# Row-tiled memory products of a query pair: tiles of 64 by 64 in place of 64 by 128

## The chip, the cores and the metric

The kernel runs on one core of one Trainium2 chip. The metric is the device time of one execution in microseconds (us). Before the change three runs took 629.06 us in the median (628.87 to 629.29).

## What is computed

Attention with a compressive memory feeds a gated feed-forward layer. There are 4 batches of 8 heads with 576 positions of 64 elements; the feed-forward layer has 2304 rows of 512, 1536 hidden units, and all weights arrive as 64-bit floats.

```python
scores = scale * np.matmul(q, k.transpose(0, 1, 3, 2))          # causal
a = softmax(scores)
local = np.matmul(a, v)
q_p = phi(q)                                                    # elu(q) + 1
mem_ret = np.einsum('bhsd,bhde->bhse', q_p, M_prev)
mem_norm = np.einsum('bhsd,bhd->bhs', q_p, z_prev)[..., None] + 1e-06
attn = g * mem_ret / mem_norm + (1 - g) * local
gate = 1.0 / (1.0 + np.exp(-(x @ w_gate)))
out = (gate * (x @ w_val)) @ w_out
```

`mem_ret` and `mem_norm` together are the memory products: 64 rows of features against 65 columns (64 of `M_prev` and one of `z_prev`) for each head.

## The kernel before

The 2304 rows go in 6 groups of 384. Four groups are the first 384 positions of one batch each; two groups (the first and the last that are worked on) are the "tails", the last 192 positions of two batches together. Each group has 4 pairs of heads, so there are 16 plain pairs and 8 tail pairs. A pair's two heads lie in SBUF partitions 0 to 63 and 64 to 127, and a product over 64 elements of one head uses only half the rows of the TensorE array. Such products run row-tiled: head 0 in the upper half of the array and head 1 in the lower half, each into its own PSUM bank. Between them the array works untiled on the products of the feed-forward layer (`matmul`, recorded on L313), on transposes (L320) and on the products with the values (`product`, L317, tiles of 128 by 64).

A row-tiled visit is one block: `scores` writes it with `pg.block()`, and all its instructions stand together in TensorE's queue. `heads` (L561) issues the score products of the visit. For one visit of each pair `more` is true; then `terms` (L518) adds the pair's memory products behind the scores, into the free columns of the same two banks. For a plain pair this is the visit `x == 0`, with one block of 128 queries against 256 keys, and memory products for three blocks of 128 queries. A tail pair's visit with `more` has two cells of 64 queries, one of each batch, each into its own half of the PSUM partitions, and its memory products are in cells of 64 queries too.

Each float32 matmul of the program stands as two matmul records with two weight loads in the trace (two passes).

After a visit DVE reads the scores of each bank with its mask and takes the row extremum (L623), ACT makes the exponentials (L635), and `recall` (L500, L504, L336 `xm`) divides the memory products by their norms. While the first plain group is in work, each hidden block's weights are turned from 64-bit floats into pairs of float32 values: `convert` loads a piece, ACT scales it (L805), DVE shifts and merges it (L807, L809, L812), ACT rounds it (L326) and DVE takes the rest (L336). There are three pieces for each of the 12 hidden blocks. Later groups load the converted weights back.

The order of all instructions comes from a planner (`Program.issue`). Each operation has an engine, an estimated cost in us and dependencies; the planner simulates the queues with these costs, and in 800 rounds of a seeded random search it moves operations that let TensorE wait in its model earlier, and keeps an order whose modelled end isn't later. The cost that a visit is given there is

```python
pe(4 * at / 2385.0 + (0.63 if more else 0.3), together, ...)
```

where `at` is the number of score columns. It costs nothing on the chip by itself; it is one input of the order.

Of the kernel before, what the change touches and what calls it, by code (L numbers as in the profile page):

```python
# [238 lines left out]
def tile_attention_memory_moe(  # L239
# [62 lines left out]
    def bank(kind):  # L302
        ids = {"att": att_banks, "gv": [3, 4], "second": [0, 1]}[kind]
        turns[kind] += 1
        t, k = banks[ids[(turns[kind] - 1) % len(ids)]]
        return t, pg.renew(k)

    def pe(cost, emit, r, w):
        pg.add("pe", cost, emit, r, w)

    def matmul(out, lhsT, rhs, n, r, w, start, stop):
        pe(0.004 + max(n, 128) / 2250.0,
           lambda: nc.tensor.matmul(out=out, lhsT=lhsT, rhs=rhs, start=start, stop=stop), r, w)  # L313
# [8 lines left out]
    def act(n, emit, r, w):  # L322
        pg.add("act", 0.09 + n / 1200.0, emit, r, w)
# [4 lines left out]
    def dve(n, emit, r, w, fast=False):  # L328
        pg.add("dve", 0.065 + n / (1920.0 if fast else 960.0), emit, r, w)
# [179 lines left out]
    def terms(u, sp, js, at):  # L509

        for c in range(3):
            cells = [(0, 128 * c, 0, 128)]
            if u.tail:
                es = (0, 1) if c == 2 else (c, c)
                cells = [(e, e * TL + (128 if c == 2 else m0), m0, m0 + 64) for e, m0 in zip(es, (0, 64))]
            for e, q, m0, m1 in cells:
                for j, r in enumerate(js):
                    nc.tensor.matmul(  # L518
                        out=sp[j][0][m0:m1, at + MC * c:at + MC * c + MC], lhsT=u.ph[r, q:q + m1 - m0],
                        rhs=mem[u.g][e][0][r, u.p, MC * j:MC * j + MC], start=True, stop=True)  # L520

    def recall(n, parts):

        u = pairs[n]
        xm, xk = xm_r.take()
        scaled(xm, [xk], parts, rn_r, 1e-6, gs[:, 2 * u.p:2 * u.p + 2], "gs")
        u.xm, u.xm_k = xm, [xk]

    def divided(u):

        return u.tail and u.n >= HP
# [24 lines left out]
    def heads(u, es, sp, js, k0, k1, at):  # L556

        for e, q, m0, m1 in es:
            kp, _ = u.kp[e]
            for j, r in enumerate(js):  # L560
                nc.tensor.matmul(  # L561
                    out=sp[j][0][m0:m1, at:at + k1 - k0], lhsT=kp[r, u.qa + q:u.qa + q + m1 - m0],
                    rhs=kp[r, u.ka + k0:u.ka + k1], start=True, stop=True)

    def scores(n, x):

        u = pairs[n]
        pair = u.tail and x == 2
        js = [slice(64 * j, 64 * j + 64) for j in range(2)]
        a = [a_r.take() for _ in js]  # L570
        if pair:
            _, q0, W = u.items[x][0]
            parts = [[(0, 0, 320)], [(0, 320, W)]]
        else:
            parts = [[(i, 0, W) for i, (_, _, W) in enumerate(u.items[x])]]
        st = [[st_r.take() for _ in js] for _ in u.items[x]]

        def part(i, cells):
            sp = [bank("att") for _ in js]
            more = pair and i == 1 or not u.tail and x == 0  # L580
            work, at = [], 0
            for y, k0, k1 in cells:
                c, q0, W = u.items[x][y]
                if pair:
                    es = [(0, 128, 0, 64), (1, 128, 64, 128)]
                    mk, mk_k = (mask2[:, :k1 - k0], "mask2") if i else (mask[:, :k1 - k0], "mask")
                else:
                    es = [(c if u.tail else 0, q0, 0, 128)]
                    mk, mk_k = mask[:, 512 - W:], "mask"
                work.append((y, es, k0, k1, at, mk, mk_k))  # L590
                at += k1 - k0
            if more:
                u.told = [(sp[j][0][:, at:at + 3 * MC].rearrange("p (c j x) -> p c j x", c=3, j=1),
                           sp[j][1], j, j + 1) for j in range(2)]

            def together():
                for _, es, k0, k1, o, _, _ in work:
                    heads(u, es, sp, js, k0, k1, o)
                if more:
                    terms(u, sp, js, at)  # L600

            with pg.block():
                if not divided(u) or pair:
                    e_ = {e for _, es, *_ in work for e, *_ in es}
                    pe(4 * at / 2385.0 + (0.63 if more else 0.3), together,
                       [u.kp[e][1] for e in e_] + (u.ph_k + [k for _, mk in mem[u.g] for k in mk] if more else []),
                       [sp[j][1] for j in range(2)])
                else:
                    (_, es, k0, k1, _, _, _), = work
                    m = k1 - k0  # L610
                    for j in range(2):
                        kq, kk, ql, kx = u.kq[j][es[0][0]]
                        keys = kq[:, u.ka + k0:u.ka + k1]
                        out, out_k = sp[j][0][:, :m], sp[j][1]
                        q = es[0][1]
                        matmul(out, kq[:, u.qa + q:u.qa + q + 128], keys, m, kk, [out_k], True, False)
                        matmul(out, ql[:, q:q + 128], keys, m, kk + kx, [out_k], False, True)
            for y, es, k0, k1, o, mk, mk_k in work:
                m = k1 - k0
                b0 = 0 if pair else sum(W for _, _, W in u.items[x][:y])  # L620
                for j in range(2):
                    (aj, ak), (sj, sk), (pj, pk) = a[j], st[y][j], sp[j]
                    dve(m + 60, lambda aj=aj, sj=sj, pj=pj, o=o, m=m, mk=mk, b=b0 + k0: nc.vector.tensor_tensor_reduce(  # L623
                        out=aj[:, b:b + m], in0=pj[:, o:o + m], in1=mk, scale=-0.125,
                        scalar=3.0e38 if i == 0 else sj[:, i - 1:i],
                        op0=ALU.add, op1=ALU.min, accum_out=sj[:, i:i + 1],
                    ), [pk, mk_k] + [sk] * (i > 0), [ak + (y,), sk])

        for i, cells in enumerate(parts):
            part(i, cells)  # L630
        u.a[x] = []
        b0 = 0
        for y, (_, _, W) in enumerate(u.items[x]):
            for (aj, ak), (sj, sk) in zip(a, st[y]):
                act(W + 120, lambda aj=aj, sj=sj, b=b0, W=W: nc.scalar.activation(  # L635
                    out=aj[:, b:b + W], in_=aj[:, b:b + W], func=AF.Exp, scale=-1.0,
                    bias=sj[:, len(parts) - 1:len(parts)],
                ), [ak + (y,), sk], [ak + (y,)])
            b0 += W
        u.a[x] = [(aj, [ak + (y,) for y in range(len(u.items[x]))], ak) for aj, ak in a]  # L640
        if u.told:
            recall(n, u.told)
            u.told = None
# [382 lines left out]
```

## Time and profile before

| | us |
|---|---|
| median of 3 runs | 629.06 |
| the profiled execution | 629.38 |
| its span | 627.5 |
| TensorE matmuls busy (PE) | 610.7 (97%) |
| weight loads busy (PEld) | 535.5 (85%) |
| VectorE (DVE) | 409.8 (65%) |
| ScalarE (ACT) | 267.5 (43%) |

The profile shows one execution. PE and PEld are TensorE's matmuls and its weight loads, which overlap. The ends of matmul records are modelled and records overlap, so what an instruction costs is read from the distance between starts. In the timeline, equal instructions that follow each other are merged into one row with their count.

### The profile page before, as it was taken

To read this page: it belongs to the slowest core of one execution; us is meant where nothing else is said; L and a number is where in the kernel's file an instruction comes from. 1 tells how busy PE (TensorE), PEld (TensorE's weight loads), DVE (VectorE), ACT (ScalarE), POOL (GpSimd) and SP (SyncE) were. 2 spreads that over 40 slices of the span, in tenths; PEclk is the share of its full clock that TensorE was granted. 3 is DMA by queue.
4 is the path that set the end of the run, shared out by engine and by line. 5 is a ranking of instruction groups with operands and counts; after the bars stand their busy time and mean duration, and the time that the engine had idled before them with its cause. 6 is when DMAs were issued, how large, how long until landed. Compare 5 with 4: busy or idle time off the path is not lost.

```text
span 627.5 us, 12396 instructions
## 1 busy us (share of the span) xinstructions
PE 610.7 (97%) x4928; PEld 535.5 (85%) x4928; DVE 409.8 (65%) x1091; ACT 267.5 (43%) x536; POOL 9.5 (2%) x51
## 2 busy tenths in 40 slices
PE   6889999998999999999999999999999999999996
PEld 3559888986898988898988898988898989999995
DVE  4999999998865568756566756678697573121211
ACT  6997667756533324333242434246363221211111
POOL 2000000000000000000000000000000000000000
PEclk9999999999999999999999999999999999999999
DMA  8667878796499699668786467978668994225351
GB/s 303 231 229 240 270 283 276 249 311 225 93 281 297 210 217 254 116 174 216 187 219 209 107 173 211 223 203 229 139 147 219 181 218 146 100 84 191 146 194 57
DMA packets 103130, 126.42 MB, mean 201 GB/s; under 512 B 79648, under 2 KB 81696, under 8 KB 95776
## 3 DMA queue, kind: packets, MB, share of 16 engines
q1 hardware_dynamic: 102928, 125.36, 69.7%
q8 instruction: 39, 0.64, 0.4%
q10 hardware_dynamic: 144, 0.26, 0.1%
q14 instruction: 19, 0.16, 0.1%
HBM read 89.43 MB, written 17.30 MB: 170 GB/s over the span
## 4 chain that ended last, share of the span: by engine, by line
PE 90%; DVE 6%; DMA 1%; ACT 1%; issue 1%; DVEq 0%; ACTq 0%
PE bank L313 72%; PE bank L317 7%; PE bank L561 6%; PE bank L320 2%; PE bank L518 2%; DVE a L623 1%; DMA wr<-in_w_dram 1%; DVE wt L809 1%; DVE wt L812 1%; ACT a L635 1%; DVE sv L336 1%; DMA kp<-in_qk_dram 1%; DVE wt L807 0%; DVE ph L492 0%; ACT wt L805 0%
## 5 line engine op out<-in xcount | busy, mean ns | idle before, releaser
L313 PE MATMUL bank<-xh,wg 128*128 128x384 f32 x576 | 163.4, 341 | 2.2 <-ACT wg L326 2.0
L313 PE MATMUL bank<-xh,sv 128*128 128x384 f32 x576 | 164.1, 341 | 0.3 <-DVE th L897 0.2
L313 PE MATMUL bank<-sv,gh 128*128 128x512 f32 x432 | 136.2, 396 | 0.3 <-ACT gh L326 0.3
L313 PEld LDWEIGHTS bank<-xh,wg 128*128 128x128 f32 x576 | 104.8, 188 | 8.8 <-ACT wg L326 2.8
L313 PEld LDWEIGHTS bank<-xh,sv 128*128 128x128 f32 x576 | 104.8, 188 | 2.8 <-DVE sv L336 0.7
L897 DVE SCALAR_TENSOR_TENSOR th<-th,bank 128x384 f32<-128x384 f32 x72 | 39.7, 551 | 98.0 <-PE bank L313 96.9
L313 PE MATMUL bank<-xl,wg 128*128 128x384 f32 x288 | 97.8, 340 | 0.0
L313 PE MATMUL bank<-xl,sv 128*128 128x384 f32 x288 | 97.6, 339 | 0.0
L313 PEld LDWEIGHTS bank<-sv,gh 128*128 128x128 f32 x432 | 79.5, 188 | 14.2 <-ACT gh L326 0.7
L895 ACT ACTIVATE th<-bank 128x384 f32<-128x384 f32 x72 | 35.3, 490 | 131.0 <-PE bank L313 130.8
L635 ACT ACTIVATE a<-a,st 128x256 f32<-128x256 f32 (+4 forms) x144 | 77.3, 581 | 26.9 <-DVE st L623 26.3
L623 DVE CUSTOM_DVE_ANT_0 a<-bank,mask 128x256 f32<-128x256 f32 (+3 forms) x144 | 64.9, 485 | 36.3 <-PE bank L561 18.3
L313 PE MATMUL bank<-sv,gl 128*128 128x512 f32 x216 | 84.8, 396 | 0.0
L326 ACT CAST gh<-th 128x384 fp32r<-128x384 f32 x72 | 36.9, 513 | 104.7 <-DVE th L897 104.5
L313 PEld LDWEIGHTS bank<-xl,wg 128*128 128x128 f32 x288 | 54.1, 188 | 4.1 <-issue 1.0
L561 PE MATMUL bank<-kp 64*128 64x256 f32 (+4 forms) x352 | 52.5, 452 | 4.0 <-DMA kp<-in_qk_dram 4.0
L653 DVE COPY at<-tl_wr 128x1024 uint16<-128x1024 uint16 (+1 forms) x72 | 46.8, 654 | 12.7 <-DMA tl_wr<-pl_wr 12.5
L313 PEld LDWEIGHTS bank<-xl,sv 128*128 128x128 f32 x288 | 54.1, 188 | 0.5
L336 DVE TENSOR_TENSOR gl<-th,gh 128x384 fp32r<-128x384 f32 x72 | 39.8, 554 | 15.5 <-ACT gh L326 15.2
L313 PEld LDWEIGHTS bank<-sv,gl 128*128 128x128 f32 x216 | 40.5, 188 | 9.4 <-DVE gl L336 0.4
L649 DVE COPY pl_wr<-a 128x1024 uint16<-128x1024 uint16 (+1 forms) x72 | 41.8, 593 | 3.8 <-ACT a L635 3.8
L561 PEld LDWEIGHTS bank<-kp 64*128 64x128 f32 (+1 forms) x352 | 23.1, 169 | 23.8 <-issue 10.5
(66 smaller groups left out, 588.0 us busy)
## 6 DMA issues: line engine op xcount, KB each, us to landing
sv<-w SPq DMA_DIRECT2D x45, 1024.0 KB, 5.4
wr<-in_w_dram SPq DMA_DIRECT2D x36, 512.0 KB, 4.6
kp<-in_qk_dram SPq DMA_DIRECT2D x32, 384.0 KB, 4.1
w<-sv SPq DMA_DIRECT2D x12, 1024.0 KB, 6.6
out_dram<-ob SPq DMA_DIRECT2D x14, 256.0 KB, 2.2
vt<-in_vp_dram SPq DMA_DIRECT2D x8, 330.0 KB, 4.8
vr<-in_vp_dram SPq DMA_DIRECT2D x8, 330.0 KB, 4.1
mb<-in_mz_dram SPq DMA_DIRECT2D x8, 260.0 KB, 3.5
```

What stands on the lines that cost most here:

```text
L313: lambda: nc.tensor.matmul(out=out, lhsT=lhsT, rhs=rhs, start=start, stop=stop), r, w)
L317: lambda: nc.tensor.matmul(out=out, lhsT=lhsT, rhs=rhs, start=start, stop=stop), r, w)
L320: pe(0.110, lambda: nc.tensor.transpose(out=out, in_=in_, identity=identity), r, w)
L326: act(n, lambda: nc.scalar.copy(out=out, in_=in_), r, w)
L336: dve(n, lambda: nc.vector.tensor_tensor(out=out, in0=in0, in1=in1, op=op), r, w)
L561: nc.tensor.matmul(out=sp[j][0][m0:m1, at:at + k1 - k0], lhsT=kp[r, u.qa + q:u.qa + q + m1 - m0], rhs=kp[r, u.ka + k0:u.ka + k1], start=Tr ...
L623: dve(m + 60, lambda aj=aj, sj=sj, pj=pj, o=o, m=m, mk=mk, b=b0 + k0: nc.vector.tensor_tensor_reduce(out=aj[:, b:b + m], in0=pj[:, o:o + m ...
L635: act(W + 120, lambda aj=aj, sj=sj, b=b0, W=W: nc.scalar.activation(out=aj[:, b:b + W], in_=aj[:, b:b + W], func=AF.Exp, scale=-1.0, bias= ...
L649: dve(2 * W, lambda: nc.vector.tensor_copy(out=pl.rearrange("p (two w) -> p two w", two=2), in_=src), r, [pk], fast=True)
L653: dve(2 * W, lambda: nc.vector.tensor_copy(out=dst, in_=tl.rearrange("p (two w) -> p two w", two=2)), [lk], [key], fast=True)
L895: act(GT, lambda: nc.scalar.activation(out=th, in_=pg_[:, :GT], func=AF.Tanh, scale=0.5), [pg_k], [th_k])
L897: dve(GT, lambda: nc.vector.scalar_tensor_tensor(out=th, in0=th, scalar=1.0, in1=pv[:, :GT], op0=ALU.add, op1=ALU.mult,), [th_k, pv_k], [t ...
```

## The change

A plain pair's visit with memory products uses cells of 64 queries. `heads` gets two cells, queries 0 to 63 into PSUM partitions 0 to 63 and queries 64 to 127 into partitions 64 to 127; `terms` does the same for each of the three blocks of 128 queries. Both cells of a block have the same right-hand operand. The planner's cost for every visit with `more`, of plain and tail pairs, goes from 0.63 to 0.8 us beside the score columns. The cells of tail pairs are not changed.

```diff
@@ def terms(u, sp, js, at):
         for c in range(3):
-            cells = [(0, 128 * c, 0, 128)]
+            cells = [(0, 128 * c + m0, m0, m0 + 64) for m0 in (0, 64)]
             if u.tail:
                 es = (0, 1) if c == 2 else (c, c)
@@ def part(i, cells):   (in scores)
                 else:
                     es = [(c if u.tail else 0, q0, 0, 128)]
+                    if more:
+                        es = [(0, q0, 0, 64), (0, q0 + 64, 64, 128)]
                     mk, mk_k = mask[:, 512 - W:], "mask"
@@ part(i, cells)
-                    pe(4 * at / 2385.0 + (0.63 if more else 0.3), together,
+                    pe(4 * at / 2385.0 + (0.8 if more else 0.3), together,
```

## Rows read from the trace of the kernel before

**Rows 1.** The page's engines, and the clock granted to TensorE in 40 slices.

```profile
PE 610.7 (97%) x4928; PEld 535.5 (85%) x4928; DVE 409.8 (65%) x1091; ACT 267.5 (43%) x536; POOL 9.5 (2%) x51
PEclk9999999999999999999999999999999999999999
```

**Rows 2.** The page's chain that ended last, by engine.

```profile
PE 90%; DVE 6%; DMA 1%; ACT 1%; issue 1%; DVEq 0%; ACTq 0%
```

**Rows 3.** Stretches: length, busy us (count) of each engine, clock, DMA share, GB/s.

```profile
44.00:140.00 96.00, 96.00 (x947) 85.04 (x947) 89.44 (x241) 66.34 (x134) 0.87 (x8) 0.98 0.79 264
140.00:150.00 10.00, 9.44 (x54) 7.24 (x52) 8.45 (x26) 6.81 (x16) 0.00 (x0) 1.00 0.64 231
150.00:167.00 17.00, 14.88 (x77) 12.25 (x77) 16.72 (x38) 8.38 (x16) 0.83 (x2) 1.00 0.46 135
167.00:400.00 233.00, 233.00 (x1749) 207.65 (x1750) 151.63 (x429) 83.81 (x179) 2.39 (x11) 1.00 0.78 204
510.00:628.00 118.00, 112.68 (x676) 104.63 (x674) 26.55 (x49) 20.60 (x40) 0.00 (x0) 0.99 0.42 138
```

**Rows 4.** What TensorE waited for from 140 to 167 us: us, times, longest.

```profile
PE bank L313 <- ACT wg L326: 2.0, 2, 1.7
```

**Rows 5.** Groups of TensorE instructions, shapes apart: the memory products' matmuls.

```profile
L518 PE MATMUL bank<-mb,ph 64*128 64x65 f32 x192 | 12.5, 263 | 0.0
...
L518 PE MATMUL bank<-mb,ph 64*64 64x65 f32 x192 | 4.9, 230 | 0.0
```

**Rows 6.** Stretches, the memory products of L518 alone: PE, PEld, clock, DMA, GB/s.

```profile
47.00:167.00 120.00, 4.69 (x72) 5.00 (x72) 1.00 0.74 247
167.00:400.00 233.00, 7.82 (x120) 8.33 (x120) 1.00 0.78 204
```

**Rows 7.** Timeline of TensorE: a plain pair's visit (start, us, instruction, count).

```profile
303.23 0.70 PE L561 MATMUL bank<-kp 64*128 64x256 f32 x4
303.76 0.78 PE L518 MATMUL bank<-mb,ph 64*128 64x65 f32 x12
304.48 0.44 PE L313 MATMUL bank<-xh,sv 128*128 128x384 f32 x1
```

**Rows 8.** Timeline of TensorE: a tail pair's visit with memory products.

```profile
478.40 0.66 PE L561 MATMUL bank<-kp 64*64 64x256 f32 x8
478.88 0.53 PE L518 MATMUL bank<-mb,ph 64*64 64x65 f32 x24
479.34 0.44 PE L313 MATMUL bank<-xh,sv 128*128 128x384 f32 x1
```

**Rows 9.** Groups of DVE instructions from 44 to 167 us: the weight conversion's.

```profile
L809 DVE SCALAR_TENSOR_TENSOR wt<-wr,wt 128x512 int32<-128x512 int32 x30 | 20.5, 684 | 0.3
L812 DVE SCALAR_TENSOR_TENSOR wt<-wr,wt 128x512 int32<-128x512 int32 x30 | 20.5, 682 | 0.1
...
L336 DVE TENSOR_TENSOR sv<-wt,sv 128x512 fp32r<-128x512 f32 x22 | 14.9, 684 | 1.0 <-ACT sv L326 1.0
L807 DVE TENSOR_SCALAR wt<-wt 128x512 int32<-128x512 int32 x30 | 12.5, 418 | 2.6 <-ACT wt L805 2.4
```

**Rows 10.** What DVE waited for from 44 to 140 us: us, times, longest.

```profile
DVE a L623 <- PE bank L518: 2.0, 4, 0.7
```

**Rows 11.** Timeline of DVE behind the plain visit at 117 us; idle time in brackets.

```profile
118.11 0.42 DVE L623 CUSTOM_DVE_ANT_0 a<-bank,mask 128x256 f32<-128x256 f32 x1 [0.73 <-PE bank L518]
```

**Rows 12.** Timeline of TensorE: the tail visit at 418 us.

```profile
418.39 0.74 PE L561 MATMUL bank<-kp 64*64 64x256 f32 x8
...
419.41 0.45 PE L313 MATMUL bank<-xl,wg 128*128 128x384 f32 x1
```

**Rows 13.** Timeline of TensorE: the tail visit at 504 us.

```profile
504.53 0.70 PE L561 MATMUL bank<-kp 64*64 64x256 f32 x5
...
505.73 0.44 PE L313 MATMUL bank<-xl,sv 128*128 128x384 f32 x1
```

**Rows 14.** The group of the value products, in tiles of 128 by 64.

```profile
L317 PE MATMUL bank<-vt,at 128*64 128x66 f32 x800 | 26.6, 226 | 0.0
```

## The prediction

> **What bounds the kernel now.** I read the page's engines and clock first: matmuls are busy for 97% of the span, and the granted clock is at its upper level (2.4 GHz) in all 40 slices [rows 1]. So a shorter stretch of TensorE is worth what rows at that clock show. The chain of waits agrees: 90% of it is TensorE [rows 2]. An average hides stages, so the stretches come next [rows 3]. From 44 to 140 us and from 167 to 400 us TensorE is busy without a gap. Between them it isn't: 9.44 of 10 us, then 14.88 of 17, together 2.7 us of waiting. There DVE is the fuller engine, 16.72 of 17 us from 150 to 167, and from 44 to 140 it has 89.44 of 96. The waits of TensorE in that part were ended above all by the rounded weights (2.0 us) [rows 4], that is by the conversion chain of which DVE does most. So there are two kinds of stage: up to 167 us TensorE and DVE are nearly level, behind it TensorE alone sets the pace to the end.
>
> **How many visits, and where.** A plain visit has 6 products, 12 matmul records. 192 records in tiles of 64 by 128 [rows 5] are thus 16 visits; the 192 in tiles of 64 by 64 are the 8 tail visits, 24 records each. By stretches, 72 records (6 visits) lie before 167 us and 120 (10 visits) behind it [rows 6]. All 16 stand before 400 us.
>
> **The price of one visit.** The trace of before shows the new shape: a tail visit with memory products has 4 score products of 64x64 over 256 keys and 12 memory products of 64x64 over 65 columns, record for record what a plain visit becomes. I compare from the visit's first matmul to the first untiled matmul behind it.
> - Plain, 64 by 128 [rows 7]: 303.23 to 303.76 is 0.53 us for the scores, 303.76 to 304.48 is 0.72 us for the memory products and the way out, 1.25 us in all.
> - Tail, 64 by 64 [rows 8]: 478.40 to 478.88 is 0.48 us, 478.88 to 479.34 is 0.46 us, 0.94 us in all.
>
> The difference is 0.31 us: 0.05 in the scores and 0.26 in the memory products. The second is the main part. The 12 records of before go as 6 steps on two tiles; the 24 of after as 6 steps on four tiles at once. I read the shorter step as the weight loads: each brings 64 columns of weights, not 128, and with only 65 columns streamed behind it a step waits for its load. The score products stream 256 columns in both forms, and there only the first loads can be shorter. The change adds no switch between tiled and untiled work: the visit is entered and left once, as before, and there is no new wait or transfer.
>
> **On the path.** 10 visits behind 167 us lie where TensorE has no gap and DVE has room (151.63 of 233 us) [rows 3]: 10 x 0.31 = 3.1 us, all of it on the path. Behind 400 us nothing of it is given back: the feed-forward products of the last group have no attention beside them, and the stretch from 510 us is TensorE's too [rows 3].
>
> 6 visits before 167 us are worth at most 6 x 0.31 = 1.9 us. What hides this part is DVE, whose work there isn't made less. It had 96 - 89.44 = 6.6 us idle from 44 to 140 us. 2.0 us of that, in 4 waits (one of them behind the last tail visit of the opening), was for visits with memory products themselves [rows 10], as the 0.73 us ahead of the mask at 118.11 [rows 11]. A plain visit that ends 0.31 us sooner shortens such a wait by that much: about 3 x 0.3 = 0.9 us that DVE surely gets back. At worst DVE is full all the same and everything is swallowed (0), at best all 1.9 us arrive. I take 1.1, a little above the sure part, since some of the other idle time in that stretch also ends with TensorE. What is late next is the rounded weights at 150 to 167 us, whose wait grows by the rest, 0.8 us.
>
> **The planner's cost.** 0.8 in place of 0.63 takes no time by itself, but 24 visits get another price and the random search can end in another order. I take 0 for it. From both sides: a better order can win at most the 2.7 us of waiting of 140 to 167 us; a worse one has its bound in the fourth rival.
>
> **Sum.** 3.1 + 1.1 = 4.2 us. The profiled execution took 629.38 us (a span of 627.5 and 1.9 around it), 0.3 above the median of the runs. 629.38 - 4.2 = 625.2; against the median, 629.06 - 4.2 = 624.9 us. I forecast 624.9. Its own range is from 624.0 (all 16 visits in full, 5.0 us) to 625.9 (nothing of the first six).
>
> **Rivals.**
> 1. *DVE swallows the first six visits.* DVE has 0.28 us idle between 150 and 167 us [rows 3], so this speaks for it; against it are DVE's waits for these very visits [rows 10]. Time: 629.06 - 3.1 = 626.0, with some tenths more if visits behind 167 us don't give all. The Trainium skill has a rule for this case, "TensorEngine Tiling (Array Packing)", section "PSUM Bottleneck": tiling makes TensorE faster but not the emptying of PSUM, which may become the limit. By that rule the gain would be the 3.1 us of the stage where DVE has room; the trace agrees with it up to 167 us and not behind.
> 2. *The new visits lose time inside.* Two of the four tail visits beside feed-forward work took longer than 0.94 us: 418.39 to 419.41 is 1.02 [rows 12], 504.53 to 505.73 is 1.20 [rows 13]. In the second the first score product starts alone and the rest come later, so I read it as a wait for the second bank, which a tail visit meets since its other scores stand directly before it. The mean of the two extra times is 0.17 us; on half of 16 visits that is 1.4 us: 629.06 - 4.2 + 1.4 = 626.3.
> 3. *The two halves can't stream the same keys at once.* In the tail each half has its own batch's keys; now both have the same. If they took turns, the score part of 0.48 us would double: 0.48 - 0.31 = 0.17 us more per visit than before, 16 x 0.17 = 2.7, 631.8 us. Against it: two of the tail's three memory blocks already share their right-hand side between the halves with no longer step, and so do the value products, 800 records in 26.6 us, 33 ns each [rows 14].
> 4. *A worse order in the conversion stretch.* One converted piece takes DVE 0.42 + 0.68 + 0.68 + 0.68 = 2.5 us [rows 9]. If the new order puts pieces behind attention work between 140 and 167 us, where DVE has no idle time, TensorE's wait for the rounded weights grows by 2.5 us for each. One piece: 627.4 us. It decides from two on (5.0 against 4.2): 629.9 us; three are 632.4. For it: the search is random and this is the tightest place. Against it: it keeps an order only if its model's end isn't later, and the cost rises by only 0.17 us a visit.
> 5. *The number of records sets the pace, not the loads.* The visit goes from 16 to 32 matmul records. The 12 memory records of before take 0.72 us, 60 ns each; 24 at that pace are 1.44 us, with the scores 0.05 shorter 0.67 us more per visit, 16 x 0.67 = 10.7, 639.8 us. The tail visit contradicts this: 24 records in 0.46 us, 19 ns each [rows 8]. The Trainium skill speaks against the change here: "TensorE: Matmul & The Clock Gate", section "Wait — 56ns, not 53.3ns?", gives about 25 ns as the least distance between matmul starts however few their columns are. By that rule 24 records would take 0.60 us before the way out, against 0.72 us with it in the plain visit, so the gain would nearly go; the trace doesn't agree.
>
> **How the numbers follow.** A measurement of this kernel tells 0.2% (1.3 us) from no change, so faster is below 627.8 and slower above 630.3. The forecast has 0.68, rival 1 0.10, rival 2 0.07: all faster, 0.85. Rival 4 with one piece or a like loss gets 0.06; it ends just below or within 0.2%, and I count it as the same. Rival 4 with two pieces or more 0.05, rival 3 0.03, rival 5 0.01: slower or close to it, 0.09. The range goes from 622.8 (all 5.0 us and about half of the waits of 140 to 167 us, by a better order) to 627.4 (one piece late), which leaves out the slower cases and a little at the fast end.
>
> **What would show it.** In the profile after, the tiles of 64 by 64 should have 192 + 16 x 24 = 576 memory records and those of 64 by 128 none. From a plain visit's first matmul to the next untiled one should be 0.94 us, with some 0.48 us before the first memory record. The clock stays at its upper level. From 167 us on, the time to the end of the span should be 3.1 us shorter, and up to 167 us about 1 us shorter with a longer wait for the rounded weights. The prediction is wrong if plain visits take over 1.1 us (rival 2 or 3), or if TensorE's idle time before 167 us changes by more than 2 us (the order).

## The result, and the profile after

The changed kernel took 621.79 us in the median of 4 runs (621.36 to 622.31), the kernel before 628.96 beside it: a ratio of 0.9893, interval 0.9879 to 0.9907. That is 7.2 us less where 4.2 were forecast, and below the range given. A second measurement on another chip of the kind, in the experiments below, gave 622.53 against 628.16 us, 0.9911 (0.9898 to 0.9923), 5.6 us.

The page after, engines and granted clock [answers to rows 1], and the chain [rows 2]:

```profile
PE 604.8 (98%) x5184; PEld 527.8 (85%) x5184; DVE 408.3 (66%) x1091; ACT 266.8 (43%) x536; POOL 9.2 (1%) x51
PEclk9999999999999999999999999999999999999999
...
PE 85%; DVE 5%; DMA 2%; ACT 2%; issue 1%; ACTq 0%; SPq 0%; DVEq 0%
```

256 records more, and 5.9 us less busy. TensorE's share of the chain is 85%, where it was 90%. The memory products after [rows 5], in tiles of 64 by 64 alone:

```profile
L518 PE MATMUL bank<-mb,ph 64*64 64x65 f32 x576 | 13.3, 218 | 0.0
```

TensorE's timeline at the plain visit that rows 7 showed, after:

```profile
297.92 0.66 PE L561 MATMUL bank<-kp 64*64 64x256 f32 x8
298.40 0.53 PE L518 MATMUL bank<-mb,ph 64*64 64x65 f32 x24
298.86 0.44 PE L313 MATMUL bank<-xh,sv 128*128 128x384 f32 x1
```

297.92 to 298.86 is 0.94 us, 0.48 and 0.46: the tail visit of before [rows 8] to the last digit. In this profile 15 of the 16 plain visits take 0.94 or 0.95 us; the first, which waits inside, takes 1.27. So the visit is priced rightly, and the surplus must come from elsewhere. The stretches after [rows 3]:

```profile
44.00:140.00 96.00, 95.60 (x1030) 83.32 (x1031) 91.83 (x254) 68.69 (x141) 1.14 (x8) 1.00 0.82 273
140.00:150.00 10.00, 9.75 (x50) 7.82 (x50) 8.96 (x17) 4.79 (x9) 0.00 (x0) 1.00 0.88 305
150.00:167.00 17.00, 14.22 (x70) 11.84 (x70) 14.57 (x33) 8.42 (x16) 0.83 (x2) 1.00 0.39 93
167.00:400.00 233.00, 232.88 (x1966) 206.52 (x1965) 151.98 (x429) 82.36 (x175) 2.62 (x11) 1.00 0.79 208
```

TensorE waits 3.0 us between 140 and 167 us, 2.7 before. What differs is the clock column of the first row: 1.00 now, 0.98 in rows 3. In stretches of 4 us, the kernel before, first, then the changed one (clock is the third number from the end):

```profile
44.00:48.00 4.00, 4.00 (x66) 3.08 (x67) 3.44 (x14) 4.00 (x9) 0.00 (x0) 0.58 0.35 105
48.00:52.00 4.00, 4.00 (x100) 3.93 (x97) 3.68 (x12) 2.56 (x6) 0.00 (x0) 1.00 0.92 323
```

```profile
44.00:48.00 4.00, 3.77 (x102) 3.60 (x104) 4.00 (x14) 3.82 (x8) 0.00 (x0) 1.00 0.90 350
```

Before, TensorE ran most of 44 to 48 us at its lower level (1.2 GHz). Ahead of it, 34.76 of the first 44 us were busy, and the last wait, 1.17 us long, ended at 43.66 us, right ahead of the fall. The first feed-forward matmul shows what the opening gained, before first, then after:

```profile
52.97 0.43 PE L313 MATMUL bank<-xh,wg 128*128 128x384 f32 x1
```

```profile
49.95 0.42 PE L313 MATMUL bank<-xh,wg 128*128 128x384 f32 x1
```

That is 3.0 us before any plain visit has run, and no tile of the change stands there: it can only come from the order and the clock. As a price the mark is a poor one, since the new order also moves work across it: the first plain visit starts at 57.22 us, later than the 56.53 of before. The idle time up to 44 us is the better sign, before first, then after:

```profile
0.00:44.00 44.00, 34.76 (x446) 21.59 (x446) 35.08 (x114) 36.29 (x71) 3.69 (x25) 1.00 0.75 266
```

```profile
0.00:44.00 44.00, 36.70 (x488) 22.95 (x488) 34.83 (x118) 37.20 (x73) 3.69 (x25) 1.00 0.76 258
```

TensorE is idle there for 7.3 us, before for 9.2: 1.9 us less. The fall adds 0.42 of 4 us, 1.7 us.

### The profile page after: what moved, and what is told of

The parts are those of the page before. It is cut to its first block, busy times and chain, and to the rows that moved or that the text cites. A ratio compares the mean times of both kernels' runs of the same rounds, so it can differ in the third digit from the quotient of the medians.

```text
span 620.1 us, 12921 instructions
## 1 busy us (share of the span) xinstructions
PE 604.8 (98%) x5184; PEld 527.8 (85%) x5184; DVE 408.3 (66%) x1091; ACT 266.8 (43%) x536; POOL 9.2 (1%) x51
## 4 chain that ended last, share of the span: by engine, by line
PE 85%; DVE 5%; DMA 2%; ACT 2%; issue 1%; ACTq 0%; SPq 0%; DVEq 0%
PE bank L313 72%; PE bank L317 6%; PE bank L561 5%; DMA wr<-in_w_dram 2%; PE bank L320 1%; DVE wt L811 1%; PE bank L518 1%; DVE a L625 1%; DVE wt L814 1%; ACT at L326 0%; DVE wt L809 0%; ACT wt L807 0%; ACT th L897 0%; ACT a L637 0%; DVE xs L336 0%
## 5 line engine op out<-in xcount | busy, mean ns | idle before, releaser
L625 DVE CUSTOM_DVE_ANT_0 a<-bank,mask 128x512 f32<-128x512 f32 (+3 forms) x144 | 64.9, 485 | 28.6 <-PE bank L561 15.2
L561 PE MATMUL bank<-kp 64*64 64x256 f32 (+4 forms) x416 | 52.0, 443 | 4.3 <-DMA kp<-in_qk_dram 4.0
L561 PEld LDWEIGHTS bank<-kp 64*64 64x64 f32 (+1 forms) x416 | 21.4, 156 | 24.4 <-issue 11.3
```

The costliest lines, as they stand in the source:

```text
L561: nc.tensor.matmul(out=sp[j][0][m0:m1, at:at + k1 - k0], lhsT=kp[r, u.qa + q:u.qa + q + m1 - m0], rhs=kp[r, u.ka + k0:u.ka + k1], start=Tr ...
```

## The experiments

Each ratio is to runs of the kernel before on the same chip.

**Tiles and cost apart.** My theory after the result: the new tiles bring what was forecast, and the order that comes with the cost of 0.8 brings the rest. The rival: the tiles bring all. Two kernels make one part of the change each. The first has the old tiles in the order of the changed kernel:

```diff
-                    pe(4 * at / 2385.0 + (0.63 if more else 0.3), together,
+                    pe(4 * at / 2385.0 + (0.8 if more else 0.3), together,
```

> Tiles as before (64 by 128), the planner's cost 0.8: the order of the changed kernel without its tiles. Theory A (tiles and order add up; the order of the opening, with the clock that fell to half at 44.6 to 48.0 us in the kernel before and not in the changed one, brings 2.5 to 3 us): about 626.3 us, the first feed-forward matmul near 49.95 us as in the changed kernel, a mean clock near 1.00. Rival B (the order is worth nothing, the tiles bring all 7): 629 us. Rival C (the weight conversion takes the opening's gain back): 628 us.

626.91 us, 0.9974 (0.9955 to 0.9992). Rival C of the expectation, 628 us, lies inside this interval. The second has both hunks with `es` and `cells` and keeps 0.63:

> Tiles of 64 by 64, the planner's cost 0.63: the order of the kernel before with the new tiles. Theory A: 624.1 to 624.9 us (16 visits of 0.31 us, of which the first six may lose up to 0.8 to DVE), the opening up to 53 us as in the kernel before with its clock dip. Rival B (the tiles bring all): 622 us. Rival of the prediction, DVE swallows the first six visits: 626.0 us.

624.96 us, 0.9951 (0.9922 to 0.9981), executions from 623.05 to 630.13. The changed kernel and this one were then run once more, beside each other:

> The changed kernel once more, beside the new tiles in the old order. Theory A (the new order is worth about 1.5 to 2 us of waits and of clock, on top of the tiles): 621.5 to 622.5 us, 2 us or more below the next kernel. Rival B (the difference to it was the chip or chance): within 1 us of it.

622.53 us, 0.9911.

> The old order with the new tiles once more. Theory A: 624 to 625 us, with executions spread over 2 us or more, as a wait of 2 us or more for the weights near 155 us lets the clock fall in some of them. Rival B: 622 us.

624.27 us, 0.9936 (0.9924 to 0.9948). The tiles alone give 0.64% (4.0 us), the order alone 0.26% (1.6 us, 0.5 to 2.8 by its interval), and 0.9936 x 0.9974 = 0.9910 is the two together: within these intervals they add up. The rival falls, if narrowly: 0.9898 to 0.9923 and 0.9924 to 0.9948 just miss each other.

The traces say where. Kernels with the same order are compared at the start of the first, the seventh and the last plain visit and at the last matmul. Old order, the kernel before, then with the new tiles, their second run (TensorE's timeline):

```profile
56.53 0.70 PE L561 MATMUL bank<-kp 64*128 64x256 f32 x4
176.78 0.70 PE L561 MATMUL bank<-kp 64*128 64x256 f32 x4
372.94 0.70 PE L561 MATMUL bank<-kp 64*128 64x256 f32 x4
622.34 0.40 PE L313 MATMUL bank<-sv,gl 128*128 128x512 f32 x1
```

```profile
55.13 0.66 PE L561 MATMUL bank<-kp 64*64 64x256 f32 x8
174.28 0.66 PE L561 MATMUL bank<-kp 64*64 64x256 f32 x8
367.66 0.66 PE L561 MATMUL bank<-kp 64*64 64x256 f32 x8
616.85 0.40 PE L313 MATMUL bank<-sv,gl 128*128 128x512 f32 x1
```

The lead is 1.40, 2.50, 5.28, 5.49 us. Six visits before 167 us brought 1.10, the nine from the seventh on 2.78 (9 x 0.31 = 2.79). The 1.40 at the first visit is no work of the tiles: the order up to there is the same, but in this execution the clock stayed at its upper level at 44 us. The changed kernel's last matmul starts another 1.62 us earlier:

```profile
615.23 0.40 PE L313 MATMUL bank<-sv,gl 128*128 128x512 f32 x1
```

So the 7.11 us between the profiles of before and after are 4.09 from the tiles (5.49 - 1.40), 1.40 from the opening in which this execution of before lost its clock, and 1.62 from the order.

That split depends on which part is changed first. In the new order (the cost alone, then the changed kernel's second run, neither with a fall) the lead is -0.41 us at the first plain visit, 1.31 at the seventh, 4.03 at the last and 5.04 at the last matmul. There the first six visits brought 1.72 us, of which 0.75 at the first: it waits inside in both, and takes 1.99 and 1.24 us. So with the fall taken off, the order is worth 0.16 us with the old tiles (622.34 - 1.40 against 620.78) and 1.1 to 1.6 us with the new ones. Each is one execution, so this shows no more than that the early visits are worth what the order lets through.

**Which part of the order.** With the new tiles, the order of the changed kernel up to its first feed-forward matmul is joined to that of before behind it, and the other way round (both searches run, then the instructions of the first part are issued, then the others in the order of the second).

```diff
-        for i in best[1]:
+        for i in first[:n] + [i for i in rest if i not in opening]:
             ops[i][3]()
```

> New tiles. The order is that of the changed kernel up to its first feed-forward matmul (some 50 us), and from there on that of the kernel before. Theory A (the order's gain is about 1 us from the opening, with fewer and shorter gaps and a smaller chance that the clock falls at 44 us, and some 0.7 us from the wait for the weights near 155 us): 623 to 623.6 us, with the single long wait of about 2 us near 155 us. Rival B (all of the order's gain lies in the opening): 622.3 us, as the changed kernel.

625.09 us, 0.9949 (0.9931 to 0.9968), slower than either expectation had it.

> New tiles. The opening's order as before, then the order of the changed kernel. Theory A: 623.2 to 624 us, the wait near 155 us in pieces of about 1.3 us and less and no fall of the clock there. Rival B: 624.3 us, as the old order with the new tiles.

623.05 us, 0.9908 (0.9891 to 0.9926). What TensorE waited for from 44 to 167 us, the new opening first, then the old one (the line numbers are those of these kernels; L330 are the feed-forward matmuls):

```profile
PE bank L330 <- ACT at L343: 2.3, 1, 2.3
PE bank L330 <- ACT wg L343: 2.0, 2, 1.7
```

```profile
PE bank L330 <- ACT gh L343: 1.3, 1, 1.3
PE bank L330 <- DVE wg L353: 0.8, 2, 0.6
PE bank L330 <- ACT wg L343: 0.8, 1, 0.8
```

The first says little of the opening: the seam made a new wait of 2.3 us. The second, with the old opening, is as low in its ratio as the changed kernel, which speaks for the part behind the opening; by the two intervals it could still be about 1 us slower. Its waits are not less in sum, 2.9 us against 2.8 for the old order with the new tiles, but they are in pieces of 1.3 us at most. In the old order the longest is one of 1.7 to 2.3 us near 155 us, and there the clock fell in some executions. The first run of the tiles alone has it, 2.26 us up to 155.30 us, and the stretch behind it shows the fall:

```profile
156.00:160.00 4.00, 4.00 (x14) 3.58 (x14) 4.00 (x9) 0.87 (x2) 0.00 (x0) 0.57 0.17 33
```

Of seven profiles with the old order behind the opening (before, the tiles alone twice, the new opening, and of the kernels below the two without shifts and the old tiles with twice the columns) four show such a fall near 155 us; of seven with the new order (after twice, the cost alone, the old opening, and below the memory tiles alone, the new tiles with twice the columns and all plain visits) none does. The mean clock of each execution is on record too. A fall takes 0.003 off it, and the stretch behind the last matmul 0.002 at most in the new order. Of the old order's 88 executions 38 have 0.997 or less, of the new order's 31 none. In the kernel before the 16 such executions have a median of 629.9 us, the other 35 one of 628.0: about 1.9 us for a fall.

But the falls are not the whole. Beside the changed kernel's second run, 5 of 6 executions with the new tiles in the old order have 0.998 or more, and their median, 624.18, is still 1.65 us above it. The two traces that differ by 1.62 us at the last matmul have no fall either; what differs there is mostly the opening, 8.9 us idle of 44 against 7.3:

```profile
0.00:44.00 44.00, 35.09 (x450) 21.84 (x454) 34.80 (x112) 36.53 (x72) 3.80 (x25) 1.00 0.76 266
```

In all, seven profiles with the old opening have 7.6 to 9.5 us of idle time up to 44 us (8.6 in the mean), seven with the new one 6.9 to 8.0 (7.5). That speaks for the opening, and the kernel with the old opening speaks against it. So the order's gain is shown as a sum; how it divides between the opening, the falls and the rest stays open.

**Is it the cost or the draw?** The planner's search is random, so the seed was changed at either cost, with the new tiles.

```diff
-        pick = random.Random(1)
+        pick = random.Random(2)
```

> The changed kernel with another seed of the planner's search, all else equal. If the cost of 0.8 itself makes the better order, it stays at 621 to 622.5 us. If the order is a draw, it can land anywhere from 620 to 626 us, and the difference lies before 167 us.

623.32 us, 0.9927 (0.9906 to 0.9948).

> New tiles, the planner's cost 0.63 as before, another seed. If the cost of 0.8 makes orders better, it stays near 624.3 us; if an order is a draw whatever the cost, it lands between 621.5 and 626 us, and 622.5 us or less would show that 0.8 isn't needed.

624.49 us, 0.9936 (0.9918 to 0.9953). With seed 3:

> The changed kernel (cost 0.8) with a third seed. If 0.8 makes the orders better as such: 621.5 to 623.5 us and at least 1 us below the next kernel. If each order is a draw: anywhere from 621 to 626 us, and either one of the pair may be lower.

624.64 us, 0.9932 (0.9916 to 0.9947).

> The new tiles at the old cost 0.63 with the third seed. If 0.8 makes the orders better as such: 624 us or more. If each order is a draw: 621 to 626 us.

625.36 us, 0.9946 (0.9929 to 0.9964). At 0.8 the three seeds give 0.9911, 0.9927 and 0.9932, at 0.63 0.9936, 0.9936 and 0.9946. The cost of 0.8 was lower in each pair, but in two of them the intervals overlap, and the seeds at one cost differ as much as the costs do. The falls don't follow the cost: of seed 3 all six executions at 0.8 and five of six at 0.63 have a mean clock of 0.997 or less, of seed 2 one and two. Among these six orders the draw is worth one or two us; whether 0.8 shifts it stays open.

**Does DVE hide the early visits?** The 36 shifts of the weight conversion (L807, 15 us of DVE) are left out of the kernel before and of the one with the new tiles at cost 0.63, at the same order.

```diff
-        dve(DM, lambda: nc.vector.tensor_scalar(
-            out=t, in0=t, scalar1=3, scalar2=None, op0=ALU.logical_shift_left), [t_k], [t_k], fast=True)
+        dve(DM, lambda: None, [t_k], [t_k], fast=True)
```

> The kernel before without the 36 shifts of the weight conversion on DVE (the weights are then not the right ones); everything else in its order and tiles. DVE has 15 us less to do, so TensorE should not wait for converted weights: 2.5 us less, 625 to 626.5 us. It is the base for the next kernel.

628.09 us, 0.9996 (0.9985 to 1.0008): nothing won.

> The same without the shifts, with the new tiles in the old order. Theory A (before 167 us DVE hides part of the first six visits): with DVE light all 16 visits count, 16 x 0.31 = 5.0 us below the kernel without shifts and with the old tiles, 620 to 621.5 us. Rival (DVE hides nothing, the visits just bring what they bring): the same distance as with the shifts, 3.5 to 4.3 us.

624.47 us, 0.9944 (0.9927 to 0.9961), 3.6 us below its base, about as with the shifts. Both expectations were wrong; the second one's rival had the distance right. In the kernel before without shifts TensorE's wait from 140 to 167 us is not shorter than in rows 4, and the chain of waits ahead of it (start, us, what) shows why:

```profile
PE bank L313 <- ACT wg L326: 2.4, 2, 2.1
```

```profile
148.97 0.70 DVE wt L811
149.68 0.02 issue
149.70 0.58 ACT sv L326
150.28 3.97 DMA wr<-in_w_dram
...
154.34 0.67 ACT wt L805
155.00 0.52 ACT wg L326
155.52 0.04 issue
155.56 1.63 PE bank L313 x4
```

The piece of weights itself is late: in the chain its load starts behind ACT's step at 149.70, as I read it when a buffer is free, takes 4 us, and ACT needs two steps behind it. With the shifts it is no other: in the kernel before, ACT's first step ahead of that wait stood still for the load (ScalarE's timeline; idle time in brackets):

```profile
156.35 0.67 ACT L805 ACTIVATE wt<-wr 128x512 f32<-128x512 f32 x1 [1.17 <-DMA wr<-in_w_dram]
```

Without shifts DVE is busy for 13.24 us of the 17 from 150 to 167 us, not 16.72 [rows 3], and the wait stays: how full DVE was didn't set it. DVE still has a hand in when the loads start: a step of it (L811 at 148.97) stands in the chain, and the queue that issues the loads waited longest for that step (without shifts, 140 to 160 us; with them it is 10.2 us):

```profile
SPq L344 <- DVE wt L811: 9.6, 3, 5.7
```

That DVE hid the early visits is not shown: 5.0 us was expected without the shifts if it did, 3.6 came, with an interval of about 1.9 to 4.6. The clock disturbs this pair, as all six executions with the new tiles have a mean clock of 0.997 or less and 7 of 11 of the base.

**What makes the visit shorter.** In the changed kernel the scores of the plain visit go back to tiles of 64 by 128, the memory products stay:

```diff
-                    if more:
-                        es = [(0, q0, 0, 64), (0, q0 + 64, 64, 128)]
```

> The changed kernel with the score products of plain visits back in tiles of 64 by 128; only the memory products are 64 by 64, so the visit changes its tiling once inside. If such a change costs as little as the step between tiles shows (nothing): 0.05 us a visit, 16 x 0.05 = 0.8, 622.6 us. If it costs as much as the way from untiled to tiled work (some 0.1 us more than a step): 16 x 0.15 = 2.4, 624.2 us.

624.47 us, 0.9934 (0.9917 to 0.9952). Its timeline:

```profile
299.90 0.70 PE L561 MATMUL bank<-kp 64*128 64x256 f32 x4
300.54 0.58 PE L518 MATMUL bank<-mb,ph 64*64 64x65 f32 x24
301.04 0.45 PE L313 MATMUL bank<-xh,sv 128*128 128x384 f32 x1
```

1.14 us, 0.20 more than the changed kernel's visit; 16 x 0.20 = 3.2 us, where the ratios differ by 0.23 to 0.41% (1.4 to 2.6 us); the visits are sure (15 of 16 take 1.14 or 1.15 us), where the rest of the 3.2 went is not known. The way to the first memory product is 0.64 us, 0.11 longer than in rows 7 with the same score tiles, and the rest 0.04 longer than with one tiling throughout. Changing the tiling inside a visit costs about 0.15 us, half of what the new tiles win, as the second of the two expectations had it.

Then the memory products got twice the columns, in either tiling; parts of the products are overwritten:

```diff
-                        out=sp[j][0][m0:m1, at + MC * c:at + MC * c + MC], lhsT=u.ph[r, q:q + m1 - m0],
-                        rhs=mem[u.g][e][0][r, u.p, MC * j:MC * j + MC], start=True, stop=True)
+                        out=sp[j][0][m0:m1, at + MC * min(c, 1):at + MC * min(c, 1) + 2 * MC], lhsT=u.ph[r, q:q + m1 - m0],
+                        rhs=mem[u.g][e][0][r, u.p], start=True, stop=True)
```

> The changed kernel with 130 streamed columns in each memory product in place of 65 (both heads' columns; the products then overwrite each other in part, so the result isn't the reference's). In tiles of 64 by 64 a step was 57 ns. If the weight load of 64 columns sets it, a step stays near 57 ns until streaming is longer, at most 60 ns; if the streamed columns set it, a step doubles to about 112 ns, the visit is 0.28 us longer.

> The kernel before with 130 streamed columns in each memory product (in part overwritten, as in the kernel with the new tiles). In tiles of 64 by 128 a step was 111 ns. If the weight load of 128 columns sets it, it stays at 111 ns and the visit at 1.25 us; if load and columns add up, it grows to about 165 ns and the visit by 0.3 us.

One execution each: 628.95 us in tiles of 64 by 64, 631.06 in tiles of 64 by 128. The timelines of the visit, new tiles first:

```profile
302.48 0.66 PE L561 MATMUL bank<-kp 64*64 64x256 f32 x8
302.96 0.84 PE L518 MATMUL bank<-mb,ph 64*64 64x130 f32 x24
303.74 0.44 PE L313 MATMUL bank<-xh,sv 128*128 128x384 f32 x1
```

```profile
303.46 0.70 PE L561 MATMUL bank<-kp 64*128 64x256 f32 x4
304.00 0.84 PE L518 MATMUL bank<-mb,ph 64*128 64x130 f32 x12
304.76 0.45 PE L313 MATMUL bank<-xh,sv 128*128 128x384 f32 x1
```

With 64 by 64 the memory part goes from 0.46 to 0.78 us; with 64 by 128 from 0.72 to 0.76. So in the old tiles the columns were hidden behind the weight loads: twice as many cost 0.04 us in all. In the new ones 65 more columns cost 0.05 us in each of the six steps: at 130 the columns set the step. With 130 columns both tilings come to nearly the same time, so a load of 128 weight columns takes about as long as 130 streamed ones. From that I infer, by halves, that a load of 64 takes about as long as streaming 65, that the new step is at both limits at once, and that smaller tiles would win nothing more here; no run has them.

Last, the other row-tiled visit of each plain pair, scores alone, in tiles of 64 by 64 too:

```diff
-                    if more:
+                    if not u.tail:
                         es = [(0, q0, 0, 64), (0, q0 + 64, 64, 128)]
```

> The changed kernel with the other row-tiled visit of each plain pair (scores alone, 512 columns) in tiles of 64 by 64 too. If only the first weight loads get shorter, 0.05 us for each of 16 visits: 0.8 us less than the changed kernel, 621.7 us. If tiles of 64 by 64 made the scores themselves faster, as they did the memory products, 0.2 us or more a visit and over 3 us less: 619 us.

621.55 us, 0.9889 (0.9871 to 0.9906). Its visit, then that of the changed kernel:

```profile
264.95 1.09 PE L561 MATMUL bank<-kp 64*64 64x384 f32 x16
265.98 0.44 PE L313 MATMUL bank<-xh,wg 128*128 128x384 f32 x1
```

```profile
264.26 1.14 PE L561 MATMUL bank<-kp 64*128 64x384 f32 x8
265.33 0.45 PE L313 MATMUL bank<-xh,wg 128*128 128x384 f32 x1
```

1.03 against 1.07 us: 0.04 a visit, some 0.7 us in all. It is the fastest kernel of the study, but its interval overlaps that of the changed kernel.

## Why the prediction was wrong

- *The visit.* Right. 0.94 us was read from the tail visits and 0.94 came, 576 records in the new tiles and none in the old. The reading that the loads set the old step held with twice the columns. Rivals 3 and 5 fell: halves that share their keys did stream at once, and the records set no pace. Of rival 2 one case is seen in the profile after: the first plain visit, entered at 57.2 us, had to wait inside. Rival 4 didn't come: no piece of the weights was late by 2.5 us.
- *The path.* Right behind 167 us: every visit counted in full, 2.78 us for nine. Before it 1.10 us came in the old order, where 1.1 were forecast, but 1.72 in the new one, so that the figure fits is in part luck. The tiles by themselves brought 4.0 us, 3.3 to 4.8 by the interval; 4.2 were forecast.
- *The reason for the early part.* Not shown, and in one point wrong: "that is by the conversion chain of which DVE does most" named the fullest engine as the cause. With 15 us less on DVE the wait stayed; what came late is the load, whose start DVE's merges have a part in.
- *The step that failed* is "The planner's cost. [...] I take 0 for it. From both sides: a better order can win at most the 2.7 us of waiting of 140 to 167 us". The order was worth 1.6 us by itself (0.5 to 2.8), which is all that the second measurement has above the 4.0 of the tiles. No reason was given for 0, and the bound was wrong in place, not in size: it left out the opening, where TensorE was idle for 9.2 of 44 us, and the clock. The order's gain was not in the sum of the waits of 140 to 167 us, which grew from 2.7 to 3.0 us. In which of the other places it lies stays open.
- *The clock.* "The granted clock is at its upper level (2.4 GHz) in all 40 slices" is what the page's digits seem to say, since 9 stands for 90% or more. The first row of rows 3 has 0.98 over 96 us; that was to be seen and was passed over. It is the one fall at 44 to 48 us, which comes and goes between executions of one order.
- *What stays open.* The two measurements gave 7.2 and 5.6 us, and the 1.5 between them is not explained: the kernel before took 0.8 us less on the second chip and the changed one 0.7 us more. Falls could be behind the first, but not behind the second, whose executions all have a mean clock of 0.998 or more. With the second measurement the time would have been 0.3 us below the range, while its gain, 5.6 us, is less than the 6.3 us at the range's fast end.

## What to carry to other kernels

Where a product streams few columns per weight load, a smaller tile can shorten the step; here it did so down to where the load and the columns seem to take equal time. Double the columns once to see which of them sets it. Take the price from a place in the same trace that already has the new shape, and count a change of tiling inside a visit as a cost. Where an order comes out of a random search, a changed cost is a new draw, worth 1.6 of 5.6 us here: measure the change at the old order too, and give the draw its own term in the range.

## What was not expected of the hardware

The granted clock fell to the lower level behind waits of 1.2 us at 44 us and of about 2 us near 155 us, in some executions of an order and not in others, and the rows behind such a fall show 0.57 and 0.58 over 4 us. Of waits near 155 us, one of 1.74 us had a fall behind it in one kernel and none in another; pieces of 1.3 us and less had none. In the two traces above a fall moved everything behind it by about 1.4 us, and in the medians of the kernel before by 1.9, as much as the order was worth. And a change from tiles of 64 by 128 to 64 by 64 inside a visit cost 0.15 us, although both are row-tiled.
